# Weight conversion in a fused attention and feed-forward kernel: two of its seven steps on GpSimd, and one chunk later at the start

## The chip, the cores and the metric

The kernel runs on one core of a Trainium2 chip. The core has a matrix engine (TensorE, PE in the profile, its weight loads PEld), a vector engine (VectorE, DVE), a scalar engine (ScalarE, ACT), a third elementwise engine (GpSimd, POOL) and a queue that here issues all DMA transfers (SyncE, SP). The engines run their own instruction streams in order and wait for each other through semaphores. PE writes to PSUM, which POOL does not touch in this kernel; everything else lives in SBUF. The metric is device time in microseconds of one execution; the median of several runs is given.

## The reference

For 8 batches, 8 heads, 576 positions and head size 64, attention with a local mask: the first four heads see the last 32 positions, the other four every fourth of the last 128. The result, laid out as 4608 tokens by 512, goes through a feed-forward layer with a leaky rectifier:

```python
scores = scale * np.matmul(q, k.transpose(0, 1, 3, 2))
scores = np.where(masks[None, :, :, :], scores, -1000000000.0)
attn = softmax(scores)
x = np.matmul(attn, v).transpose(0, 2, 1, 3).reshape(B * S, H * D)
h = x @ w_in                                        # 512 -> 2048
g = np.maximum(h, 0.0) + alpha * np.minimum(h, 0.0)
return (g @ w_out).astype(np.float32)               # 2048 -> 512
```

q, k, v and alpha are 32-bit floats. The weights `w_in` and `w_out` reach the kernel as 64-bit words: each weight is stored as a double.

## The kernel before

**Precision.** Every large product is done as three products of a split operand: a value is cast to the matrix engine's 32-bit format (its high part), and the rest (its low part) is value minus high part. `PASSES` pairs high with high, high with low, low with high.

**Weights.** There are 32 chunks, 16 columns blocks of 128 of `w_in` and 16 row blocks of `w_out`. A chunk is 128 partitions by 512 weights, and arrives as 128 × 1024 32-bit words. `load_weight` issues its transfer, from the SP queue, into one of a few staging buffers. A `Conversion` then makes the 32-bit float and its two parts:

- `magnitude` (line 335): ACT takes the absolute value of the upper word, read as a float (line 342).
- `words` (line 344), four instructions of DVE: a clamp to the range of exponents that can be represented (line 348), a shift and mask (350), the upper word's sign and exponent bits brought in (352), the lower word's bits brought in (354). The last of them frees the staging buffer for the next load.
- `high` (line 358): ACT casts into the high weight tile (line 360).
- `low` (line 362): DVE subtracts (line 363) into the low weight tile.

**Order.** The order in which instructions are emitted is written out by hand, and it is the order in each engine's stream. The list `wq` fixes in which order the chunks are loaded and converted: `load()` and `conversion()` take the next one.

**The head** (lines 820 to 892). Attention is done by pairs of heads; a `Pair` has scores on PE, `maxima` on DVE (line 216: PSUM plus mask into SBUF with the row maximum), exponentials on ACT (228), `divisions` on DVE (235 to 238), transposes on PE, copies on ACT (255), values on PE, and `highs` on ACT (302) and `lows` on DVE (307) that split the result. The loop over s does the first four pairs, one per pass, with one chunk converted in each: words interleaved with the second half of the maxima. A chunk's magnitude comes one pass ahead of its words.

**The first stage** (n = 0 to 7, line 904). Step n does the feed-forward of the first 512 tokens for one block of 128 hidden values: `ffn_h` (PE, line 375), `ffn_relu` (ACT, 383 and 384), `ffn_sum` (DVE, 389), `ffn_high` (ACT, 402), `ffn_low` (DVE, 407), `ffn_y` (PE, 422), beside the attention of one more pair over two steps. Up to two chunks a step are converted: `now` holds the chunks whose words come in this step, `late` those whose low part does. The tuples with eight entries say how many chunks are taken and loaded in each step.

**The second stage** (n from 8, line 974) has the next 512 tokens and the rest of the first 512, one chunk a step, until the last one at about step 22. There the first sums of weights (`combine`, lines 466 and 469, the only work on POOL before the change apart from setting constants) follow in emission order; they serve the later stages, which use combined weights (`Four`, `phase_h`, `phase_y`) and convert nothing.

Of the kernel before, what the change touches and what calls it, by code (L numbers as in the profile page):

```python
# [9 lines left out]
F32 = mybir.dt.float32  # L10
F32R = mybir.dt.float32r
U32 = mybir.dt.uint32
AF = mybir.ActivationFunctionType
ALU = mybir.AluOpType
# [34 lines left out]
F64_LOW = float.fromhex("0x1p-15")  # L49
F64_HIGH = float.fromhex("0x1.dffffep16")  # L50
# [7 lines left out]
def tile_window_attention_prelu_ffn(  # L58
# [11 lines left out]
    nc = tc.nc  # L70
# [256 lines left out]
    class Conversion:  # L327
# [7 lines left out]
        def magnitude(self):  # L335
            i = self.index
            if NC <= i < 2 * CUT and i % 2 == 0:
                self.a = spare_a[i // 2 % 2]
            else:
                self.a = ffp.tile([P, DM], U32, tag="m", name=f"wa{self.id}", bufs=5)  # L340

            nc.scalar.activation(out=self.a.bitcast(F32), in_=self.st[:, :, 1].bitcast(F32), func=AF.Abs)

        def words(self):
            a, af = self.a, self.a.bitcast(F32)
            lo, hi = self.st[:, :, 0], self.st[:, :, 1]
            return [
                lambda: nc.vector.tensor_scalar(
                    out=af, in0=af, scalar1=F64_LOW, scalar2=F64_HIGH, op0=ALU.max, op1=ALU.min),
                lambda: nc.vector.tensor_scalar(  # L350
                    out=a, in0=a, scalar1=3, scalar2=0x3FFFFFFF, op0=ALU.logical_shift_left, op1=ALU.bitwise_and),
                lambda: nc.vector.scalar_tensor_tensor(  # L352
                    out=a, in0=hi, scalar=0xC0000000, in1=a, op0=ALU.bitwise_and, op1=ALU.bitwise_or),
                lambda: nc.vector.scalar_tensor_tensor(
                    out=a, in0=lo, scalar=29, in1=a, op0=ALU.logical_shift_right, op1=ALU.bitwise_or),
            ]
# [3 lines left out]
            nc.scalar.copy(out=self.dst[0], in_=self.a.bitcast(F32))  # L360

        def low(self):
            nc.vector.tensor_tensor(  # L363
                out=self.dst[1], in0=self.a.bitcast(F32), in1=self.dst[0].bitcast(F32), op=ALU.subtract)


# [3 lines left out]
    def ffn_h(t, f, first=0, end=NC):  # L370
        if first == 0:
            ms[t, f] = bank("a", [P, TT], f"h_{t}_{f}")
        for c in range(first, end):
            for n, (a, e) in enumerate(PASSES):
                nc.tensor.matmul(  # L375
                    ms[t, f], lhsT=weight(0, a, f)[:, c * P:(c + 1) * P], rhs=half(t, c)[:, e, :],
                    start=(c == 0 and n == 0), stop=(c == NC - 1 and n == 2))

    def ffn_relu(t, f):

        ps = ms[t, f]
        m = ffp.tile([P, TT], F32, tag="m", name=f"m_{t}_{f}", bufs=5)
        nc.scalar.activation(out=m, in_=ps, func=AF.Relu, scale=-1.0)
        nc.scalar.activation(out=ps, in_=ps, func=AF.Relu)
        ms[t, f] = ps, m
# [23 lines left out]
    def ffn_y(t, f):  # L409
        first = (t, f) in ((0, 0), (0, CUT), (1, 0), (2, CUT))  # L410
        if first:
            ys[t] = [bank("y", [P, TT], f"y_{t}_{f}_{c}") for c in range(NC)]
        g = gs.pop((t, f))
        cut, rest = (t, f) == (0, CUT - 1), t == 0 and f == NF - 1
        last = cut or (t, f) in ((0, NF - 1), (1, NF - 1), (2, CUT - 1))
        if last:
            o = [ffp.tile([P, TT], F32, tag="m", name=f"ob_{t}_{f}_{c}", bufs=5) for c in range(NC)]
        for c in range(NC):
            if rest:
                nc.sync.dma_start(out=o[c], in_=part[c])  # L420
            for n, (a, e) in enumerate(PASSES):
                nc.tensor.matmul(  # L422
                    ys[t][c], lhsT=weight(1, a, f)[:, c * P:(c + 1) * P], rhs=g[:, e, :],
                    start=(first and n == 0), stop=(last and n == 2),
                )
        if not last:
            return
        for c in range(NC):
            if rest:
                nc.vector.tensor_tensor(out=o[c], in0=ys[t][c], in1=o[c], op=ALU.add)  # L430
            elif c % 2:
                nc.vector.tensor_copy(out=o[c], in_=ys[t][c])
            else:
                nc.scalar.copy(out=o[c], in_=ys[t][c])  # L434
            nc.sync.dma_start(
                out=part[c] if cut else outT[c * P:(c + 1) * P, t * TT:(t + 1) * TT], in_=o[c])
# [373 lines left out]
    def load():  # L810
        if loads:
            load_weight(*loads.pop(0))

    def conversion():

        w = Conversion(*convs.pop(0))
        w.magnitude()
        return w
# [15 lines left out]
    for s in range(NC):  # L834
        u = pairs[s]
        pairs[s + NC].load_qk()
        load()
        if s == 0:
            u.maxima()
            u.exponentials(0, 3)  # L840
            w = conversion()
            u.exponentials(3)
            nc.vector.tensor_scalar_mul(nal, al, -1.0)
            nc.vector.tensor_scalar(out=bal, in0=al, scalar1=-1.0, scalar2=1.0, op0=ALU.mult, op1=ALU.add)
            for op in w.words():
                op()
        else:
            u.maxima(w.words())
            u.exponentials()
            pairs[s - 1].highs()  # L850
        w.high()
        u.divisions()
        if s + 1 == NC:
            ffn_h(0, 0, 0, 2)
        u.transposes()
        later = conversion()
        u.copies()
        if s + 2 <= NC:
            pairs[s + 2].scores()
        if s:  # L860
            pairs[s - 1].lows()
        w.low()
        w = later
        u.values()
        pairs[s + NC].load_v()
    u, v = pairs[NC - 1], pairs[NC]
# [3 lines left out]
    now = [conversion(), conversion()]  # L870
# [12 lines left out]
    ffn_relu(0, 0)  # L883
    v.exponentials(4)
    ffn_relu(0, 1)
    for _ in range(3):
        load()
    late, now = now, [conversion(), conversion()]
    for w in late:
# [7 lines left out]
    for p in range(2 * NC, AHEAD):  # L897
        n = EARLY + 2 * (p - 2 * NC)
# [5 lines left out]
    for n in range(CUT):  # L904


        scored, valued, turned = score_at.get(n), value_at.get(n), turn_at.get(n)
        words = [op for ops in zip(*(w.words() for w in now)) for op in ops]
        if scored:
            scored.scores()  # L910
        if valued:
            valued.values()
        if n + 1 == CUT:
            ffn_y(*slices[n - 1])
        if n == 0:
            for f in range(2):
                ffn_sum(*slices[f])
        elif turned:
            ffn_sum(*slices[n])
        ffn_high(*slices[n])  # L920
        if turned:
            turned.divisions()
        for w in late:
            w.low()
        if scored:
            scored.maxima([lambda: ffn_low(*slices[n])] + words)
            ffn_h(*slices[n + 1])
            scored.exponentials(0, 4)
            valued.highs()
            scored.exponentials(4)  # L930
            valued.lows()
        else:
            if valued:
                valued.highs()
                valued.lows()
            if n:
                ffn_h(*slices[n + 1])
            ffn_low(*slices[n])
            for op in words[:4]:
                op()  # L940
        following = None
        if turned:
            following = [conversion() for _ in range((2, 2, 2, 1, 0, 0, 1, 1)[n])]
            if n:

                ffn_relu(*slices[n + 1])
                ffn_sum(*slices[n + 1])
            for op in words[4:]:
                op()
        elif not scored:  # L950
            for op in words[4:]:
                op()
        late = now
        for _ in range((2, 2, 1, 0, 0, 1, 1, 1)[n]):
            load()
        if not turned and n < CUT - 1:
            ffn_relu(*slices[n + 1])
        if turned:
            turned.transposes()
            turned.copies()  # L960
        for w in late:
            w.high()
        now = following if turned else [conversion() for _ in range((2, 2, 2, 1, 0, 0, 1, 1)[n])]
        if 0 < n < CUT - 1:
            ffn_y(*slices[n - 1])
    ffn_relu(*slices[CUT])
# [2 lines left out]
    for k in range(NFP):  # L969
        n = SECOND + 1 + 2 * k + (2 if k > 1 else 0)  # L970
# [3 lines left out]
    for n in range(CUT, NS):  # L974
        scored, valued, divided, turned = (at.get(n) for at in (score_at, value_at, divide_at, turn_at))
# [3 lines left out]
        if n <= SECOND - 2:  # L979
# [17 lines left out]
            late, now = now, [conversion()] if convs else []  # L997
# [115 lines left out]
```

## Time and profile before

| What | Value |
|---|---|
| median of 3 runs | 919.5 us (919.32 to 920.11) |
| the profiled execution's own time | 919.12 us |
| its span in the trace | 917.3 us |
| PE busy | 869.6 us, 95% of the span |
| DVE busy | 549.4 us, 60% |
| ACT busy | 428.1 us, 47% |
| POOL busy | 48.8 us, 5% |
| mean granted TensorE clock | 0.978 |

A profile of this kind shows one execution. The span runs from the first to the last instruction; the execution's own time is 1.8 us longer. Busy shares are means over stages that differ: the conversions end before a quarter of the span is over.

### The profile page before, as it was taken

How to read it: one execution, taken by the hardware profiler on the slowest of the kernel's cores; microseconds unless marked ns; L12 is line 12 of the kernel's file. 1: busy time of each engine (PE TensorE's matmuls, PEld its weight loads, DVE VectorE, ACT ScalarE, POOL GpSimd, SP SyncE). 2: the span in 40 equal slices, each digit the busy share in tenths (PEclk: the TensorE clock that was granted, in tenths of full speed). 3: DMA queues.
4: the chain of work that ended last, by engine and by line, in shares of the span. 5: the costliest groups of instructions: out<-in, count | busy, mean ns of one | idle time of the engine just before them, and what ended most of it. 6: DMA issues, size and time to landing. Idle time of an engine off the chain costs nothing.

```text
span 917.3 us, 20648 instructions
## 1 busy us (share of the span) xinstructions
PE 869.6 (95%) x8080; PEld 714.5 (78%) x8080; DVE 549.4 (60%) x1607; ACT 428.1 (47%) x1250; POOL 48.8 (5%) x54
## 2 busy tenths in 40 slices
PE   4668999979999998999999999999999999999998
PEld 4556888868877886888778877887888888888886
DVE  6999487686766675676345746673347627503731
ACT  6776455453535444365445543554456306303610
POOL 0000000030222541000000000000000000000000
PEclk9879999999999998999999999999999999999999
DMA  9842152216798984475557656665466456435641
GB/s 334 295 138 70 47 189 93 91 53 202 253 305 268 305 277 152 145 209 163 174 176 200 172 179 192 201 173 155 150 165 182 145 161 195 137 103 157 183 132 46
DMA packets 101313, 159.83 MB, mean 174 GB/s; under 512 B 8416, under 2 KB 47456, under 8 KB 101216
## 3 DMA queue, kind: packets, MB, share of 16 engines
q1 hardware_dynamic: 101216, 158.51, 55.8%
q8 instruction: 64, 1.05, 0.5%
q14 instruction: 33, 0.27, 0.1%
HBM read 124.92 MB, written 33.55 MB: 173 GB/s over the span
## 4 chain that ended last, share of the span: by engine, by line
PE 87%; DVE 7%; ACT 2%; DMA 1%; issue 1%; SPq 1%; DVEq 0%; ACTq 0%
PE y L705 28%; PE pA L567 14%; PE h L375 14%; PE y L422 13%; PE pC L567 7%; PE pB L567 4%; PE o L266 3%; PE s L192 3%; PE t L248 2%; DMA ws<-w_in 1%; ACT w_dt.float L228 1%; DVE w_dt.float L216 1%; DVE w_dt.float32r L363 1%; DVE wa L352 0%; DMA w_dt.uint<-w_out 0%
## 5 line engine op out<-in xcount | busy, mean ns | idle before, releaser
L375 PE MATMUL h<-x,w_dt.float32r 128*128 128x512 f32 x576 | 150.7, 414 | 7.3 <-DVE nm L216 6.9
L422 PE MATMUL y<-g,w_dt.float32r 128*128 128x512 f32 x576 | 140.7, 393 | 0.0
L375 PEld LDWEIGHTS h<-x,w_dt.float32r 128*128 128x128 f32 x576 | 114.2, 201 | 33.0 <-issue 7.3
L422 PEld LDWEIGHTS y<-g,w_dt.float32r 128*128 128x128 f32 x576 | 106.6, 188 | 22.4 <-ACT ob L434 0.4
L705 PE MATMUL y<-gp,ring_w 128*128 128x512 f32 x480 | 113.7, 392 | 0.0
L705 PE MATMUL y<-gp,ring_xA 128*128 128x512 f32 x444 | 104.7, 391 | 1.0 <-issue 1.0
L705 PEld LDWEIGHTS y<-gp,ring_w 128*128 128x128 f32 x480 | 89.3, 188 | 18.6
L705 PEld LDWEIGHTS y<-gp,ring_xA 128*128 128x128 f32 x444 | 82.8, 188 | 18.4 <-issue 1.1
L228 ACT ACTIVATE pr<-pr,nm 128x64 f32<-128x64 f32 (+1 forms) x240 | 80.1, 335 | 28.7 <-DVE nm L216 28.7
L609 ACT COPY stage<-pA 128x512 f32<-128x512 f32 x72 | 42.3, 587 | 104.3 <-PE pA L567 104.3
L402 ACT CAST g<-m 128x512 fp32r<-128x512 f32 x48 | 29.8, 621 | 72.5 <-DVE m L397 66.2
L635 DVE TENSOR_TENSOR gp<-n,gp 128x512 fp32r<-128x512 f32 x96 | 63.2, 684 | 0.0
L627 DVE SCALAR_TENSOR_TENSOR n<-n,bal,stage 128x512 f32<-128x512 f32 x72 | 53.9, 749 | 13.9 <-ACT n L623 13.1
L567 PE MATMUL pA<-parts_w,ring_w 128*128 128x512 f32 x234 | 57.7, 390 | 0.0
L631 ACT CAST gp<-n 128x512 fp32r<-128x512 f32 x96 | 56.6, 615 | 1.9 <-DVE n L627 1.9
L567 PE MATMUL pA<-parts_w,ring_xA 128*128 128x512 f32 x228 | 56.2, 390 | 0.5 <-ACT raw_xB L302 0.5
L705 PE MATMUL y<-gp,ring_g 128*128 128x512 f32 x228 | 55.0, 393 | 0.0
L216 DVE CUSTOM_DVE_ANT_0 pr<-s,mask_sb 128x64 f32<-128x64 f32 (+1 forms) x288 | 45.0, 213 | 16.3 <-PE s L192 15.2
L623 ACT ACTIVATE n<-stage 128x512 f32<-128x512 f32 x72 | 45.6, 633 | 12.5 <-DVE stage L616 12.0
L567 PEld LDWEIGHTS pA<-parts_w,ring_w 128*128 128x128 f32 x234 | 43.8, 188 | 9.1
L728 DVE TENSOR_TENSOR ob<-y,py 128x512 f32<-128x512 f32 x24 | 16.4, 691 | 57.4 <-PE y L705 57.4
L567 PEld LDWEIGHTS pA<-parts_w,ring_xA 128*128 128x128 f32 x228 | 42.7, 188 | 9.5 <-ACT raw_xB L302 0.6
(104 smaller groups left out, 1213.5 us busy)
## 6 DMA issues: line engine op xcount, KB each, us to landing
ring_w<-wS SPq DMA_DIRECT2D x68, 256.0 KB, 2.8
ring_xA<-wS SPq DMA_DIRECT2D x67, 256.0 KB, 2.8
v<-vW SPq DMA_DIRECT2D x24, 576.0 KB, 3.9
ring_w<-wO SPq DMA_DIRECT2D x40, 256.0 KB, 2.8
ring_xA<-wO SPq DMA_DIRECT2D x37, 256.0 KB, 2.7
out<-ob SPq DMA_DIRECT2D x36, 256.0 KB, 3.2
ring_g<-wS SPq DMA_DIRECT2D x33, 256.0 KB, 2.8
wO<-w_dt.float32r SPq DMA_DIRECT2D x32, 256.0 KB, 5.2
```

The lines of the kernel that those rows point to most:

```text
L216: nc.vector.tensor_tensor_reduce(out=self.pr[rows, r, :], in0=self.ps[e][rows, g, :], in1=mask_sb[rows, kind, :], scale=-SCALE, scalar=3.0 ...
L228: nc.scalar.activation(out=self.pr[rows, r, :], in_=self.pr[rows, r, :], func=AF.Exp, bias=self.nm[rows, r:r + 1], scale=-1.0, accum_out=s ...
L375: nc.tensor.matmul(ms[t, f], lhsT=weight(0, a, f)[:, c * P:(c + 1) * P], rhs=half(t, c)[:, e, :], start=(c == 0 and n == 0), stop=(c == NC ...
L402: nc.scalar.copy(out=g[:, 0, :], in_=ms[t, f])
L422: nc.tensor.matmul(ys[t][c], lhsT=weight(1, a, f)[:, c * P:(c + 1) * P], rhs=g[:, e, :], start=(first and n == 0), stop=(last and n == 2),)
L567: nc.tensor.matmul(to, lhsT=w[:, (2 * a + c) * P:(2 * a + c + 1) * P], rhs=part_of(name, e)[:, c * TT:(c + 1) * TT], start=start and c == ...
L609: nc.scalar.copy(out=self.s(n), in_=self.A)
L623: nc.scalar.activation(out=self.m[n], in_=self.at(n), func=AF.Relu, scale=-1.0)
L627: nc.vector.scalar_tensor_tensor(out=self.m[n], in0=self.m[n], scalar=bal[:, f:f + 1], in1=self.at(n), op0=ALU.mult, op1=ALU.add)
L631: nc.scalar.copy(out=self.g(n)[:, 0], in_=self.m[n])
L635: nc.vector.tensor_tensor(out=g[:, 1], in0=self.m.pop(n), in1=g[:, 0].bitcast(F32), op=ALU.subtract)
L705: nc.tensor.matmul(ys2[tt], lhsT=w[:, k * P:(k + 1) * P], rhs=g[:, e], start=j == 0 and n == 0, stop=j == GF - 1 and n == 2)
```

## The change

The clamp moves from `words` into `magnitude` and from DVE to POOL, so that it is issued right behind the absolute value; `words` has three instructions now, and slices such as `words[:4]` and `words[:2]` cut at other places in the sequence. The subtraction of the low part moves from DVE to POOL. In the head, pass s = 0 converts nothing any more: chunk 0's magnitude is the one that pass 0 issues for the next pass, and every later chunk of the head and of steps 0 to 2 comes one place later. Step 3 takes two chunks instead of one. One load that was issued ahead of step 0 is issued later, and step 2 issues two loads instead of one, so that from step 4 on the numbers are as before.

```diff
-            nc.scalar.activation(out=self.a.bitcast(F32), in_=self.st[:, :, 1].bitcast(F32), func=AF.Abs)
+            af = self.a.bitcast(F32)
+            nc.scalar.activation(out=af, in_=self.st[:, :, 1].bitcast(F32), func=AF.Abs)
+            nc.gpsimd.tensor_scalar(
+                out=af, in0=af, scalar1=F64_LOW, scalar2=F64_HIGH, op0=ALU.max, op1=ALU.min)
...
             return [
-                lambda: nc.vector.tensor_scalar(
-                    out=af, in0=af, scalar1=F64_LOW, scalar2=F64_HIGH, op0=ALU.max, op1=ALU.min),
...
         def low(self):
-            nc.vector.tensor_tensor(
+            nc.gpsimd.tensor_tensor(
                 out=self.dst[1], in0=self.a.bitcast(F32), in1=self.dst[0].bitcast(F32), op=ALU.subtract)
...
         if s == 0:
             u.maxima()
-            u.exponentials(0, 3)
-            w = conversion()
-            u.exponentials(3)
+            u.exponentials()
             nc.vector.tensor_scalar_mul(nal, al, -1.0)
             nc.vector.tensor_scalar(out=bal, in0=al, scalar1=-1.0, scalar2=1.0, op0=ALU.mult, op1=ALU.add)
-            for op in w.words():
-                op()
         else:
             u.maxima(w.words())
             u.exponentials()
             pairs[s - 1].highs()
-        w.high()
+            w.high()
...
         if s:
             pairs[s - 1].lows()
-        w.low()
+            w.low()
...
-    for _ in range(3):
+    for _ in range(2):
         load()
...
-            following = [conversion() for _ in range((2, 2, 2, 1, 0, 0, 1, 1)[n])]
+            following = [conversion() for _ in range((2, 2, 2, 2, 0, 0, 1, 1)[n])]
...
-        for _ in range((2, 2, 1, 0, 0, 1, 1, 1)[n]):
+        for _ in range((2, 2, 2, 0, 0, 1, 1, 1)[n]):
             load()
...
-        now = following if turned else [conversion() for _ in range((2, 2, 2, 1, 0, 0, 1, 1)[n])]
+        now = following if turned else [conversion() for _ in range((2, 2, 2, 2, 0, 0, 1, 1)[n])]
```

More of the change, by code (lines that the diff above doesn't have):

```diff
@@ L340, in magnitude @@
                 self.a = ffp.tile([P, DM], U32, tag="m", name=f"wa{self.id}", bufs=5)
-            nc.scalar.activation(out=self.a.bitcast(F32), in_=self.st[:, :, 1].bitcast(F32), func=AF.Abs)
+            af = self.a.bitcast(F32)
+            nc.scalar.activation(out=af, in_=self.st[:, :, 1].bitcast(F32), func=AF.Abs)
+            nc.gpsimd.tensor_scalar(
+                out=af, in0=af, scalar1=F64_LOW, scalar2=F64_HIGH, op0=ALU.max, op1=ALU.min)
         def words(self):
-            a, af = self.a, self.a.bitcast(F32)
+            a = self.a
             lo, hi = self.st[:, :, 0], self.st[:, :, 1]
             return [
-                lambda: nc.vector.tensor_scalar(
-                    out=af, in0=af, scalar1=F64_LOW, scalar2=F64_HIGH, op0=ALU.max, op1=ALU.min),
                 lambda: nc.vector.tensor_scalar(
```

## The prediction

> **What bounds the kernel now.** I read the table of busy time by stretch first, because a mean over 917 us hides stages with different limits, then who waited for whom, the chain that ended last inside the stretches that mattered, and the timeline there. The columns of the table: stretch, its length, then busy us and count for PE, PEld, DVE, ACT, POOL, the granted PE clock, DMA share, GB/s.
>
> ```profile
> core 0 of [0], span 917.3 us
> core 0: us, PE busy (x) PEld busy (x) DVE busy (x) ACT busy (x) POOL busy (x), PEclk, DMA share, GB/s
> 21.00:28.00 7.00, 4.29 (x150) 3.65 (x149) 6.20 (x36) 5.98 (x27) 0.00 (x0) 0.92 1.05 388
> 43.00:92.00 49.00, 37.19 (x548) 30.27 (x549) 46.16 (x155) 34.81 (x110) 0.00 (x0) 0.82 0.30 100
> 106.00:183.00 77.00, 77.00 (x368) 63.18 (x360) 58.02 (x102) 40.29 (x75) 0.00 (x0) 1.00 0.38 125
> 183.00:203.00 20.00, 15.30 (x200) 12.28 (x200) 17.62 (x56) 9.16 (x34) 7.08 (x6) 0.95 0.12 31
> ```
> ```profile
> PE h L375 <- DVE nm L216: 5.0, 2, 3.2
> ```
>
> Four stages concern the change, all before 204 us, where the last chunk is converted. In the head (one row of it, 21 to 28) DVE is busy 6.20 of 7.00 us and ACT 5.98. From 43 to 92 DVE is the limit: 46.16 of 49 us, while PE has 12 us of gaps, two of them (5.0 us) because a matmul had to wait for the row maxima of line 216. From 106 to 183 PE has no gap: what DVE saves there is worth nothing, and DVE's 19 us of slack is what may be lost unseen. From 183 to 203 PE has gaps of 4.7 us again. POOL does nothing until 192.
>
> **What is removed, added and moved.** For each of 32 chunks the clamp and the low part go from DVE to POOL; one conversion leaves pass s = 0 of the head, and everything behind it is one chunk later until step n = 3 takes two chunks and catches up. No transfer is added; of the SP queue, one of the three loads ahead of step 0 goes behind it, and one of step 3's into step 2. In each step a load still waits for the same words as before, one chunk earlier in number, so no transfer is newly exposed. The prices of DVE's part, on the chain of the head (start, length, what):
>
> ```profile
> 5.82 8.20 DMA ws<-w_in
> 14.05 0.67 ACT wa L342
> 14.72 0.58 ACT pt L255 x2
> 15.30 3.32 ACT w_dt.float L228 x20
> ...
> 25.89 0.19 DVE rs L235
> ...
> 28.15 0.60 DVE w_dt.float32r L363
> 29.75 0.34 DVE wa L348
> ...
> 33.13 0.19 DVE rs L235
> ```
>
> A clamp takes 0.34 us of the path and a low 0.60, so a chunk frees DVE for 0.94 us. *Head.* A pass lasts 33.13 − 25.89 = 7.24 us, and both pieces lie on its chain. Without them it is 6.3, and ACT's share of the pass (5.98/7.00 × 7.24 = 6.2) becomes nearly equal, so I take a full 0.95 us for each of the passes s = 2 and 3: 1.9 us. The two POOL instructions of a pass fall after the cast of line 360, while DVE subtracts out of PSUM (line 307) or starts its maxima (scores in PSUM), so I charge no contention here. If that cover is missing it costs up to what is gained.
>
> Ahead of that, the first pass. Before, the conversion of chunk 0 stood in it, and chunk 1's magnitude waited at 14.05 for its weights, 8.20 us after their issue; the copies and the 3.32 us of exponentials stood behind it on ACT.
>
> ```profile
> 10.47 0.19 ACT L228 ACTIVATION_READ_ACCUMULATOR w_dt.float<-w_dt.float,nm 64x1 f32 x1
> 10.79 0.17 DVE L235 TENSOR_SCALAR rs<-sums 128x10 f32<-128x10 f32 x1
> ...
> 12.08 1.30 PE L248 MATMUL t<-ident,w_dt.float 128*128 128x128 f32 x5 [0.86 <-DVE w_dt.float L238]
> ```
>
> After, the last exponential ends one magnitude earlier (10.66 − 0.67 ≈ 10.0) and DVE has no words left to finish, so the division starts near 10.05 instead of 10.79. The transposes then end at 13.38 − 0.75 ≈ 12.6, the copies at 13.25, the 3.32 us of exponentials at 16.6; before they ended at 15.30 + 3.32 = 18.62. The magnitude that now stands between is chunk 0's, whose words DVE had finished by 10.79 before, so its weights are there. That is 2.0 us, and DVE (maxima and three words, about 3.3 us from 11.35) is done by then. Here the cost moves: the next pieces of DMA, later in the queue, had no wait before and are asked for 2 to 4 us sooner; with the queues full (388 GB/s) one of them may become late. Sum of the head: 2.0 + 1.9 = **3.9 us** (bounds 1.5, if the transfers pace it, and 4.6).
>
> *43 to 92, the first stage.* The rows of lines 348 and 363 in this stretch (busy us and count in DVE):
>
> ```profile
> 43.00:92.00 49.00, 3.54 (x9) 0.82 0.30 100
> ```
> ```profile
> 43.00:92.00 49.00, 7.80 (x12) 0.82 0.30 100
> ```
>
> Nine clamps and twelve lows leave: 9 × 0.34 + 12 × 0.60 = 10.3 us of DVE. What they cost on POOL: the trace has no POOL clamp and no POOL subtraction with this output, so by the nearest rows:
>
> ```profile
> 299.75 2.54 POOL L466 TENSOR_TENSOR wsum_xA<-w_dt.float32r 128x512 f32<-128x512 f32 x2 [8.60 <-DVE wc L479]
> ```
> ```profile
> masks.py:199 POOL TENSOR_SCALAR_AFFINE_SELECT ident<-ident 128x128 f32<-128x128 f32 x1 | 0.3, 292 | 0.1
> masks.py:197 POOL MEMSET ident<- 128x128 f32 x1 | 0.2, 204 | 0.3 <-POOLq L1106 0.3
> L1106 POOL MEMSET const-bfloat16-1.0<- 128x1 bf16 x1 | 0.1, 101 | 0.0
> ```
>
> A two-input POOL instruction of this shape takes 1.27 us: the low. The clamp has one input: the memset, stretched by its slope from one column to 128, gives 0.10 + 4 × 0.10 = 0.5, the floor; the affine select, which does arithmetic, 0.10 + 4 × 0.19 = 0.87; the two-input row 1.27 is the ceiling. I take 0.87. What decides is not that POOL is slower but what it does to DVE beside it, and the trace shows that once:
>
> ```profile
> 192.97 1.52 DVE L348 TENSOR_SCALAR wa<-wa 128x512 f32<-128x512 f32 x1
> 194.53 1.39 DVE L350 TENSOR_SCALAR wa<-wa 128x512 uint32<-128x512 uint32 x1
> 195.84 1.21 DVE L407 TENSOR_TENSOR g<-m,g 128x512 fp32r<-128x512 f32 x1
> 196.97 1.21 DVE L352 SCALAR_TENSOR_TENSOR wa<-ws,wa 128x512 uint32<-128x512 uint32 x1
> 198.21 1.09 DVE L354 SCALAR_TENSOR_TENSOR wa<-ws,wa 128x512 uint32<-128x512 uint32 x1
> ```
> ```profile
> 192.66 2.98 POOL L466 TENSOR_TENSOR wsum_xB<-w_dt.float32r 128x512 f32<-128x512 f32 x2 [191.36 <-PE t L248]
> 195.72 4.18 POOL L469 TENSOR_TENSOR wsum_xB<-wsum_xB 128x256 f32<-128x256 f32 x4
> ```
> ```profile
> 195.76 0.30 PE L192 MATMUL s<-k,q 64*32 64x64 f32 x2
> 200.75 1.30 PE L192 MATMUL s<-k,q 64*32 64x64 f32 x70 [4.70 <-DVE m L397]
> ```
>
> Five DVE instructions that take some 2.5 us alone (0.34, 0.34, three of 0.60) needed 6.33 us, from 192.97 to 199.30, while POOL ran without a gap; POOL's pair took 2.98 instead of 2.54. So DVE loses (6.33 − 2.5)/6.33 = 0.6 us for each us of POOL beside it. All five read and write SBUF alone. The Trainium skill ("SBUF — State Buffer", section "Who interferes with whom") says that a DVE instruction with two SBUF inputs, or a one-input one in its two-port mode, takes the port pair that GpSimd uses, that the holder keeps it for the whole instruction and the other waits. The trace agrees that they exclude each other (a clamp of 0.34 took 1.52); it differs in the price, as DVE lost 0.6 of POOL's time and not all of it.
>
> Instructions with an operand in PSUM I take as free of this (none stands beside POOL in those rows). Their busy time from 58 to 75, lines 216, 307 and 389:
>
> ```profile
> 58.00:75.00 17.00, 2.18 (x24) 0.90 0.35 119
> ```
> ```profile
> 58.00:75.00 17.00, 0.89 (x3) 0.90 0.35 119
> ```
> ```profile
> 58.00:75.00 17.00, 1.48 (x2) 0.90 0.35 119
> ```
>
> That is 4.6 us of DVE's 17; without clamps and lows (3.8) some 13 remain, of which 65% contend. POOL's time there, slowed as the pair above (1.49 a low, about 1.0 a clamp): 9 × 1.0 + 12 × 1.49 = 26.9 us; 26.9 × 0.65 × 0.6 = 10.5 us lost against 10.3 saved. On top, the words of one chunk more fall into this stage, as the head has one chunk fewer (step 4 gets two instead of one): 0.34 + 2 × 0.60 = 1.5 us of DVE, of which I charge 1.0, since DVE has 2.8 us idle in the stage. Sum of the stage: **−1.2 us**. Bounds: +6 if POOL meets mostly maxima, −11 if DVE is blocked at nearly every POOL instruction.
>
> *106 to 183.* DVE has 19 us spare over 14 chunks, 1.4 us each, and gets 0.94 more against 2.5 × 0.6 = 1.5 us lost at most. Nothing.
>
> *183 to 203.* Here POOL's order matters. The sums of line 466 are the first thing in POOL's queue now and start as soon as their buffer is free, at 192.66, beside the words of the last chunk; PE then waits 4.70 us for line 397 behind them. After the change POOL must do the last chunk's low first, and that waits for the high part, which waits for exactly those words. So the sums can't start before the words are over. DVE gains the 3.8 us lost above, and 0.34 + 0.34 + 0.60 from clamps and low; against it one low part of 1.27 us blocks the shift of the last chunk by about 1.2. I get 3.8 + 1.3 − 1.2 = 3.9, near PE's gap of 4.7, and take **3.8 us** (bounds 2.0 and 4.7). The sums then run some 5 us later, beside maxima and PSUM work, and are needed two steps later: nothing.
>
> Sum: 3.9 − 1.2 + 3.8 = 6.5 us off the profiled execution's own 919.12 (span 917.3): 912.6. The runs' median, 919.5, lies 0.4 above it, so **913.0 us**.
>
> **Rivals.** *Blocked for the whole instruction*: uncontended POOL time 9 × 0.87 + 12 × 1.27 = 23.1 us × 0.65 = 15 us lost against 10.3, and 1.0: −5.7; the head stays, the last stage gives 3.2. Net 1.4: 918.1. For it: the clamp's row of 1.52. Against: the two-input rows, 1.1 to 1.2. The rule of the Trainium skill cited above would have it so.
>
> *Slower.* The same place, with a dear clamp: if POOL needs 1.49 for it too and the lows come just when DVE does words (casts finish right after a chunk's words, so its low meets the next chunk's), then POOL works 21 × 1.49 = 31.3 us, all of it beside contending work: 31.3 × 0.6 = 18.8 lost, 10.3 saved, 1.0 more: −9.5; with 7.7 from head and end that is 1.8 us slower, about 921.5. It decides from a loss of 7.7 us in the first stage on, which is 0.37 us for each of its 21 moved instructions beyond what the move saves. Against it: each scored step has twelve maxima of 0.2 us under which POOL can run.
>
> *The stage gains too.* If lows and clamps fall mostly under maxima, 43 to 92 gives 6 us instead of losing: 905.5. For it: POOL starts a low as soon as the cast ends, and maxima follow the casts in every other step.
>
> *It doesn't do what it says*: DVE would wait for clamps at its first word if POOL lay behind. A clamp is issued most of a step before its word; I fold it into the slower case.
>
> **Chances and range.** Forecast 0.56 (909 to 916.5 by the bounds of head and end), whole-instruction blocking 0.18, slower 0.12, gain in the stage too 0.14. What can be told from no change is 0.2%, 1.8 us. Faster: 0.56 + 0.14 and a third of 0.18, 0.76; within: 0.11, the middle of the blocking case; slower: 0.13. The range goes from 905 to 920, with both outer cases' near ends.
>
> **What would show it.** Right: the division of pair 3 near 29.3 instead of 33.13; no wait of ACT for the second weights; line 350, 352 and 354 longer than 0.6 to 1.2 us beside POOL and unchanged elsewhere; the first sums of line 466 after 195 us, and PE's wait of 4.70 us below 1.5. Wrong: a POOL clamp above 1.3 us, first-stage steps longer than 8.5 us, or PE gaps between 106 and 183. The forecast falls if 43 to 92 loses more than 4 us.

## The result, and the profile after

The changed kernel takes 927.93 us (median of 5 runs, 925.69 to 931.3), the kernel before 919.5 us beside it (5 runs): a ratio of 1.0095, 95% interval 1.0067 to 1.0122. The forecast was 913.0 us, with a range up to 920. It is slower by 8.4 us where 6.5 us of gain were forecast. The profiled execution is the fastest of the five: 925.69 us, span 923.9 us, against 919.12 and 917.3 before, so the trace shows 6.6 us of the loss. Medians here and below are over all executions; the ratios leave out one, of the kernel with the clamp on DVE, which took 4835.98 us where its other three took 908.98 to 911.12.

The table of busy time by stretch, after the change, over the same stretches as in the prediction (length, then busy us and count of PE, PEld, DVE, ACT, POOL, granted clock, DMA share, GB/s):

```profile
21.00:28.00 7.00, 4.04 (x108) 3.44 (x116) 6.01 (x27) 4.42 (x18) 2.14 (x3) 1.00 1.05 390
43.00:92.00 49.00, 33.95 (x383) 26.96 (x383) 42.91 (x107) 30.17 (x96) 28.84 (x18) 0.72 0.31 98
106.00:183.00 77.00, 77.00 (x405) 63.39 (x404) 52.83 (x73) 41.13 (x81) 38.15 (x23) 0.99 0.34 112
183.00:203.00 20.00, 20.00 (x157) 16.36 (x156) 14.78 (x45) 12.37 (x36) 10.39 (x7) 1.00 0.25 83
```

From 43 to 92 us PE does less than before (33.95 us instead of 37.19), and so does DVE (42.91 instead of 46.16). DVE gets 107 instructions done there and not 155, at 0.40 us each in the mean instead of 0.30, and is idle for 6.1 us instead of 2.8. So two things may be at work: something makes DVE wait, and something makes its instructions longer. From 106 to 183 PE still has no gap. The last row lies earlier in the work than it did before, because the same steps now come later.

Four marks that both traces have cut the difference into parts: the division of pair 3 at the end of the head; the first matmul of the scores in step 20, ahead of the last chunk's stage; the same for the next pair's scores behind that stage; and the end of the span. (Starts in us, as the view of the chain gives them; the last four rows of the table are the lengths between.)

| | before | after | difference |
|---|---|---|---|
| pair 3's division | 33.13 | 33.41 | +0.3 |
| scores of step 20 | 183.21 | 195.25 | +12.0 |
| scores behind the last chunk | 216.31 | 223.90 | +7.6 |
| end of the span | 917.3 | 923.9 | +6.6 |
| head | 33.13 | 33.41 | +0.3 |
| first stage and on to step 20 | 150.08 | 161.84 | **+11.8** |
| last chunk's stage | 33.10 | 28.65 | **−4.4** |
| the rest | 701.0 | 700.0 | −1.0 |

So the end of the conversions gave about what was forecast (4.4 us, 3.8 forecast), and the loss lies in front of it. What is new there is on POOL. The groups of the two moved instructions, by shape (count, busy us, mean ns; then POOL's idle time before them):

```profile
L344 POOL TENSOR_SCALAR wa<-wa 128x512 f32<-128x512 f32 x26 | 52.9, 2035 | 74.6 <-ACT wa L343 74.6
L364 POOL TENSOR_TENSOR w_dt.float32r<-wa,w_dt.float32r 128x512 fp32r<-128x512 f32 x26 | 35.1, 1350 | 4.1 <-ACT w_dt.float32r L361 4.1
```

The clamp takes 2.04 us, half as long again as the subtraction with its two inputs. And DVE waits for it, 17.8 us in all up to 215 us, of which 5.8 lie between 20 and 106 us (the view of waits: who for whom, us, times, longest):

```profile
DVE wa L351 <- POOL wa L344: 17.8, 16, 1.7
```

How that looks once in the head, first on POOL and then on DVE (start, length):

```profile
19.14 1.92 POOL L344 TENSOR_SCALAR wa<-wa 128x512 f32<-128x512 f32 x1 [6.39 <-ACT wa L343]
21.02 1.27 POOL L364 TENSOR_TENSOR w_dt.float32r<-wa,w_dt.float32r 128x512 fp32r<-128x512 f32 x1
```
```profile
21.09 1.49 DVE L351 TENSOR_SCALAR wa<-wa 128x512 uint32<-128x512 uint32 x1 [1.47 <-POOL wa L344]
```

DVE stands still for 1.47 us, until the clamp ends. Then POOL starts the subtraction that stood behind the clamp, 0.07 us before DVE starts the shift, and the shift takes 1.49 us instead of 0.42. The chain of waits goes through POOL here, where POOL did nothing at all in the kernel before (start, length, whose):

```profile
26.50 0.58 ACT wa L343
...
27.16 1.93 POOL wa L344
...
34.88 0.57 ACT wa L343
...
35.53 1.92 POOL wa L344
37.44 1.23 POOL w_dt.float32r L364
38.67 2.06 POOL w_dt.float L344
40.73 1.89 POOL wa L344
```

In the last chunk's stage the prediction nearly holds. POOL must do the chunk's low part first, and the sums of weights (now line 467) start after the words are over; PE, then, waits 1.60 us and not 4.70 for the split behind those words, and the 12 matmuls of `h` that follow take 3.04 us where they took 4.16 (after on POOL and PE, then PE before):

```profile
208.97 1.27 POOL L364 TENSOR_TENSOR w_dt.float32r<-wa,w_dt.float32r 128x512 fp32r<-128x512 f32 x1 [2.94 <-ACT w_dt.float32r L361]
210.19 2.98 POOL L467 TENSOR_TENSOR wsum_xB<-w_dt.float32r 128x512 f32<-128x512 f32 x2
```
```profile
209.68 0.95 PE L192 MATMUL s<-k,q 64*32 64x64 f32 x70 [1.60 <-DVE m L398]
210.71 3.04 PE L376 MATMUL h<-x,w_dt.float32r 128*128 128x512 f32 x12
```
```profile
201.98 4.16 PE L375 MATMUL h<-x,w_dt.float32r 128*128 128x512 f32 x12
```

### The profile page after: what moved, and what is told of

Its sections match the earlier page's. It is cut to its first block, busy times and chain, and to the rows that moved or that the text cites. A ratio compares the mean times of both kernels' runs of the same rounds, so it can differ in the third digit from the quotient of the medians.

```text
span 923.9 us, 20689 instructions
## 1 busy us (share of the span) xinstructions
PE 876.3 (95%) x8080; PEld 719.5 (78%) x8080; DVE 549.5 (59%) x1543; ACT 430.1 (47%) x1250; POOL 154.4 (17%) x118
## 4 chain that ended last, share of the span: by engine, by line
PE 84%; DVE 5%; ACT 3%; POOL 2%; issue 2%; DMA 2%; SPq 0%; DVEq 0%; ACTq 0%; POOLq 0%
PE y L706 28%; PE pA L568 14%; PE h L376 12%; PE y L423 12%; PE pC L568 7%; PE pB L568 4%; PE o L266 4%; PE s L192 2%; POOL wa L344 2%; PE t L248 1%; DMA w_dt.float<-kT 1%; DMA ws<-w_in 1%; DVE w_dt.float L353 1%; DVE wa L353 1%; POOL w_dt.float L344 1%
## 5 line engine op out<-in xcount | busy, mean ns | idle before, releaser
L376 PE MATMUL h<-x,w_dt.float32r 128*128 128x512 f32 x576 | 152.6, 418 | 6.2 <-DVE nm L216 3.4
L706 PEld LDWEIGHTS y<-gp,ring_xA 128*128 128x128 f32 x444 | 82.8, 188 | 18.1 <-issue 0.9
L344 POOL TENSOR_SCALAR wa<-wa 128x512 f32<-128x512 f32 x26 | 52.9, 2035 | 74.6 <-ACT wa L343 74.6
L628 DVE SCALAR_TENSOR_TENSOR n<-n,bal,stage 128x512 f32<-128x512 f32 x72 | 54.0, 749 | 13.9 <-ACT n L624 13.3
L729 DVE TENSOR_TENSOR ob<-y,py 128x512 f32<-128x512 f32 x24 | 16.4, 691 | 57.4 <-PE y L706 57.4
```

The lines of the kernel that those rows point to most:

```text
L344: nc.gpsimd.tensor_scalar(out=af, in0=af, scalar1=F64_LOW, scalar2=F64_HIGH, op0=ALU.max, op1=ALU.min)
L376: nc.tensor.matmul(ms[t, f], lhsT=weight(0, a, f)[:, c * P:(c + 1) * P], rhs=half(t, c)[:, e, :], start=(c == 0 and n == 0), stop=(c == NC ...
L628: nc.vector.scalar_tensor_tensor(out=self.m[n], in0=self.m[n], scalar=bal[:, f:f + 1], in1=self.at(n), op0=ALU.mult, op1=ALU.add)
L706: nc.tensor.matmul(ys2[tt], lhsT=w[:, k * P:(k + 1) * P], rhs=g[:, e], start=j == 0 and n == 0, stop=j == GF - 1 and n == 2)
```

## The experiments

Three causes were on the table. **A**: the clamp on POOL is dear, and its length lies on the path between absolute value and shift. **B**: the subtractions block DVE, as the prediction's rival "blocked for the whole instruction" had it. **C**: the new order, one chunk later, is at fault. Times are medians, each ratio is against the kernel before on the same chip, with its 95% interval.

### One part at a time

The changed kernel with only the clamp back on DVE:

```diff
-            nc.gpsimd.tensor_scalar(
-                out=af, in0=af, scalar1=F64_LOW, scalar2=F64_HIGH, op0=ALU.max, op1=ALU.min)
...
             return [
+                lambda: nc.vector.tensor_scalar(
+                    out=af, in0=af, scalar1=F64_LOW, scalar2=F64_HIGH, op0=ALU.max, op1=ALU.min),
```

> The changed kernel with the clamp back on DVE as the first of four words; the low parts stay on POOL and the chunks one place later. Theory A (the POOL clamp's own time, 1.92 us, makes DVE wait at the shift behind it, 17.8 us in all, and that is the loss): the first stage gets back most of its 12 us, the sums behind the last chunk stay late, so 912 to 917. Theory B (POOL's lows block DVE's words, whatever the clamp does): still above 923. Theory C (the later order of chunks costs the time): about 926.

911.0 us, ratio 0.9896 (0.9876 to 0.9916): 17 us faster than the changed kernel. B alone is out: all 32 subtractions on POOL make the kernel faster.

The changed kernel with only the subtraction back on DVE:

```diff
-            nc.gpsimd.tensor_tensor(
+            nc.vector.tensor_tensor(
                 out=self.dst[1], in0=self.a.bitcast(F32), in1=self.dst[0].bitcast(F32), op=ALU.subtract)
```

> The changed kernel with the low parts back on DVE; only the clamp is on POOL. Theory A: 922 or more, and DVE still waits for the clamp ahead of line 351, about 15 us. Theory B: 914 to 918, as nothing with two inputs runs on POOL beside the words any more, and shifts are back near 0.42 us. Theory C: about 926.

924.77 us, ratio 1.0048 (1.0032 to 1.0064). The clamp alone costs, and the wait is there without any subtraction on POOL:

```profile
DVE wa L351 <- POOL wa L344: 14.5, 15, 1.8
```

Both edits together, so that the new order alone is left:

> Clamp and low both back on DVE; what is left of the change is the order, one chunk later. Theories A and B: 2 to 3 us faster than before, 916.5 to 918, from the first pass of the head (its division already stands near 9.8 instead of 10.8, the second pass's near 16.4 instead of 18.6). Theory C: 922 or more.

919.06 us, ratio 0.9992 (0.9979 to 1.0006). C is out: the order by itself costs nothing. By the end it gives nothing that can be told from no change either, where 2 to 3 us were expected. And the other way about, both parts on POOL in the old order (the kernel before with the changed kernel's `magnitude`, `words` and `low`):

> The kernel before with clamp and low moved to POOL and the old order of chunks kept. Theories A and B: the first pass's gain is missing as well, 929 to 932. Theory C: 915 to 918, the gain of the move without the loss of the order.

930.16 us, ratio 1.0111 (1.0081 to 1.0141). That is the changed kernel's ratio within the two intervals, so the new order isn't what makes the move dear.

The start of step 20's scores makes a table of the four ways to place the two parts, all in the new order, each from one trace:

| | clamp on DVE | clamp on POOL |
|---|---|---|
| low part on DVE | 182.55 | 188.87 (+6.3) |
| low part on POOL | 179.72 (−2.8) | 195.25 (+12.7) |

The two edits don't add: −2.8 and +6.3 would make +3.5, and it is +12.7, 9.2 us more. That is taken up again below.

### How long the clamp is

If A holds, the time must follow the clamp's length. Three kernels change that alone. One leaves the upper limit out, so that the instruction has one operation instead of two; one clamps only 200 of the 512 columns and leaves 312 as they are; one does the whole clamp in two instructions of 256 columns.

```diff
-                out=af, in0=af, scalar1=F64_LOW, scalar2=F64_HIGH, op0=ALU.max, op1=ALU.min)
+                out=af, in0=af, scalar1=F64_LOW, scalar2=None, op0=ALU.max)
```

> The changed kernel with half a clamp: POOL's instruction has only the lower limit (the upper limit is left out). If the price of a POOL clamp goes by its operations, it falls from 1.92 to about 1 us, DVE's wait ahead of the shift all but goes, and the time is 912 to 918. If it goes by elements alone, 1.9 us and 925 to 929 as with the full clamp.

```diff
-                out=af, in0=af, scalar1=F64_LOW, scalar2=F64_HIGH, op0=ALU.max, op1=ALU.min)
+                out=af[:, :200], in0=af[:, :200], scalar1=F64_LOW, scalar2=F64_HIGH, op0=ALU.max, op1=ALU.min)
```

> The changed kernel with the POOL clamp over the first 200 of 512 columns alone (the other 312 are left unclamped), which should bring its price down to about the 0.87 us that the prediction took. If the price of the clamp is the one term that was mis-sized, the rest of the prediction's sum holds: 911 to 915, and DVE's wait ahead of the shift falls from 17.8 us to under 4. If having any POOL instruction between magnitude and shift is the trouble (a handover more, or the block by the low behind it), 919 or more.

```diff
-                out=af, in0=af, scalar1=F64_LOW, scalar2=F64_HIGH, op0=ALU.max, op1=ALU.min)
+                out=af[:, :256], in0=af[:, :256], scalar1=F64_LOW, scalar2=F64_HIGH, op0=ALU.max, op1=ALU.min)
+            nc.gpsimd.tensor_scalar(
+                out=af[:, 256:], in0=af[:, 256:], scalar1=F64_LOW, scalar2=F64_HIGH, op0=ALU.max, op1=ALU.min)
```

> The changed kernel with each POOL clamp as two instructions of 256 columns. What the clamp's price is made of: if a fixed part dominates, each half takes well over 0.96 us and the pair over 2.4; if columns do, 1.0 each and about 2.0 for the pair, and the time stays within 2 us of the changed kernel's 928. No theory expects a gain.

The groups of the clamp by shape, one operation, 200 columns, and the two halves:

```profile
L344 POOL TENSOR_SCALAR wa<-wa 128x512 f32<-128x512 f32 x26 | 43.2, 1662 | 81.3 <-ACT wa L343 78.2 <-ACT w_dt.float32r L360 3.1
```
```profile
L344 POOL TENSOR_SCALAR wa<-wa 128x200 f32<-128x200 f32 x26 | 25.1, 967 | 92.4 <-ACT wa L343 79.4 <-DVE nm L216 7.7 <-DVE x L307 5.2
```
```profile
L344 POOL TENSOR_SCALAR wa<-wa 128x256 f32<-128x256 f32 x26 | 32.1, 1234 | 69.7 <-ACT wa L343 57.9 <-DVE nm L216 6.7 <-DVE x L307 5.2
...
L346 POOL TENSOR_SCALAR wa<-wa 128x256 f32<-128x256 f32 x26 | 27.9, 1074 | 0.0
```

| clamp on POOL | mean us of it | median us | ratio |
|---|---|---|---|
| 200 of 512 columns | 0.97 | 911.57 | 0.991 (0.9891 to 0.9928) |
| one operation | 1.66 | 921.55 | 1.0025 (1.0012 to 1.0038) |
| the changed kernel | 2.04 | 927.93 | 1.0095 (1.0067 to 1.0122) |
| two halves | 1.23 + 1.07 | 929.21, one run | |

The clamp with one operation came out between the two cases that were expected, 1 us and 1.9. In the kernel with 200 columns DVE's wait for clamps fell to 8.0 us and not under 4, but 7.5 of them lie between 106 and 183 us, where PE is full.

The time follows the length: from 0.97 to 2.04 us it grows by 16.4 us, 15 us for each us of a clamp. POOL does 14 clamps between 20 and 92 us in the changed kernel (the groups of that stretch):

```profile
L344 POOL TENSOR_SCALAR wa<-wa 128x512 f32<-128x512 f32 x8 | 16.1, 2011 | 16.5 <-ACT wa L343 16.5
...
L344 POOL TENSOR_SCALAR w_dt.float<-w_dt.float 128x512 f32<-128x512 f32 x6 | 12.5, 2090 | 20.2 <-ACT w_dt.float L343 20.2
```

So with the subtractions on POOL as well, it is as if every clamp of head and first stage lay on the path with its whole length. That is a description and no mechanism: with the subtractions on DVE, a clamp of some 2 us on POOL adds 5.7 us to the time (919.06 to 924.77), under 3 us for each us. With the clamp of 0.97 us, near the 0.87 that the prediction assumed, the kernel is at 911.6 us, where 913.0 was forecast.

### Where the clamp costs

Clamps of the first 18 chunks on DVE, of the last 14 on POOL, all subtractions on POOL:

```diff
+            if i >= 18:
+                self.clamp(nc.gpsimd)
...
+            first = [] if self.index >= 18 else [lambda: self.clamp(nc.vector)]
```

> The changed kernel with the clamp on POOL only for the last 14 chunks, those converted while PE has no gaps; the first 18 clamp on DVE. If the loss lies in the first stage alone and DVE's slack later takes the waits, 911 to 913 (the last chunk's clamp may cost 1 to 2 us, as its shift waited 1.2 us in the changed kernel). If a POOL clamp of 1.92 us costs wherever it stands, 917 or more.

911.15 us, ratio 0.9917 (0.9896 to 0.9937), as with no clamp on POOL at all (911.0). DVE waits for these clamps three quarters as long as in the changed kernel:

```profile
DVE wa L357 <- POOL wa L349: 13.3, 10, 1.4
```

Of these 13.3 us 12.2 lie between 106 and 183 us, where PE is full, and cost nothing. Of the 17.8 us of the changed kernel, 8.2 lie between 106 and 183 us and are free for the same reason. The sum of a wait over a whole trace says little; its place decides.

### The last chunk's low part alone

The kernel before, with one of its 32 subtractions on POOL, the last:

```diff
-            nc.vector.tensor_tensor(
+            (nc.gpsimd if self.index == 2 * NF - 1 else nc.vector).tensor_tensor(
```

> The kernel before with one single instruction moved: the low part of the last chunk goes to POOL, in front of the sums of line 466 in POOL's queue. If holding back those sums is what the last stage gains, PE's gap of 4.7 us ahead of 201 us falls to about 1.5 and the time is 3 us shorter, 916 to 917.5, with nothing changed before 183 us. If the gain needs the other lows off DVE too, less than 1 us: 919 to 920.

913.59 us, ratio 0.9941 (0.9921 to 0.9961). One moved instruction holds back the sums of line 466, and PE's wait falls from 4.70 to 1.18 us. The order on POOL and, behind the wait, PE with `h` at 3.01 us instead of 4.16:

```profile
196.56 1.27 POOL L363 TENSOR_TENSOR w_dt.float32r<-wa,w_dt.float32r 128x512 fp32r<-128x512 f32 x1 [195.26 <-ACT w_dt.float32r L360]
197.78 2.99 POOL L466 TENSOR_TENSOR wsum_xB<-w_dt.float32r 128x512 f32<-128x512 f32 x2
```
```profile
197.26 0.95 PE L192 MATMUL s<-k,q 64*32 64x64 f32 x70 [1.18 <-DVE m L397]
198.29 3.01 PE L375 MATMUL h<-x,w_dt.float32r 128*128 128x512 f32 x12
```

By the scores behind the stage the kernel is 4.9 us ahead (211.46 against 216.31). That is the prediction's last term, shown by itself, and more than the 3 us that were expected. The median lies 6.4 us under the 920.0 of the kernel before; for what goes beyond the 4.9 no run shows a cause.

### Why the head gave nothing

With the clamp on DVE, the copies of the first pair's transposes started 2.6 us sooner, at 12.07 us, sooner even than was forecast. But the first values product (line 266) did not follow. The kernel before, then the changed kernel with its clamp on DVE:

```profile
16.07 2.14 PE L266 MATMUL o<-pt,w_dt.float 64*64 64x32 f32 x72 [1.25 <-ACT w_dt.float L228]
```
```profile
16.29 2.14 PE L266 MATMUL o<-pt,w_dt.float 64*64 64x32 f32 x72 [2.39 <-ACT w_dt.float L228]
```

The view names ACT as the releaser, with a wait that is longer now though ACT was sooner. The operand left over is the pair's values, which come by DMA; no view names their transfer here. To see whether it is them, the first weight chunk's load was moved behind the loads that this product needs:

```diff
-    load()
...
+    load()
```

(one line, from ahead of the second pair's q and k to behind them and the first pair's values; the rest as with the clamp on DVE)

> The kernel with the clamp on DVE and the lows on POOL, and the load of chunk 0 issued behind those of pair 1 and of pair 0's values. In all runs so far the first product with the values starts at 15 to 16.3 us, whether its other operand is ready at 13 or at 15.3; if the full transfer queue sets that, it starts near 14.7 now, the head ends 1 to 1.4 us sooner, and the time is 909.5 to 910.5. If not, 911 as without the reordering, or 1 us more if chunk 0's weights become late.

908.29 us, ratio 0.9889 (0.9869 to 0.9909), and the product starts 1.6 us sooner:

```profile
14.68 2.15 PE L266 MATMUL o<-pt,w_dt.float 64*64 64x32 f32 x72 [0.49 <-ACT w_dt.float L228]
```

Pair 3's division comes at 29.93 us instead of 31.10. In the traces of all the kernels that load in the old order the product starts between 15.06 and 16.29 us, whenever the copies end. So 14.68 lies outside, but how much of the 1.6 us is the moved load is not shown; nor is it separated whether it is the values or the second pair's q and k, which moved up too. That transfers hold up this product, and the head with it, is what fits best; they come at 390 GB/s in the first table's row. This is the lowest median found, 1.1% under the kernel before, with the subtractions on POOL and the clamps on DVE; its interval overlaps that of the same kernel with the loads in the old order.

### Why the two parts together cost 9 us more

Two ideas were tried. The first: POOL starts a subtraction just as its clamp releases the shift (21.02 and 21.09 us above), so the collision is built in. Here every subtraction is issued right behind its cast and the clamps behind the subtractions:

```diff
+        def clamp(self):
+            af = self.a.bitcast(F32)
...
         for w in late:
             w.high()
+            w.low()
...
+        for w in now:
+            w.clamp()
```

> The changed kernel with both parts on GpSimd, but each chunk's subtraction issued on GpSimd right behind the cast that it follows, ahead of the clamps that follow in the list, so that no subtraction stands directly behind the clamp that releases a shift. Theory that the extra 9 us of the two parts together come from the subtraction that GpSimd starts just as its clamp releases VectorE's shift: a part of it comes back, a mean shift well under the 1.25 us of the changed kernel and 919 to 924 us. Rival, that only the length of VectorE's wait for its clamps counts: the clamps come later behind the subtractions, the wait grows from 17.8 us, and the time is 928 us or more.

945.86 us, ratio 1.0291 (1.0264 to 1.0318). The collision at the shift is gone, a shift of the main group (the 26 chunks with their floats in `wa`) takes 0.49 us and not 1.25, but the wait grows from 17.8 to 57.4 us:

```profile
DVE wa L354 <- POOL wa L347: 47.3, 21, 3.3
...
DVE w_dt.float L354 <- POOL w_dt.float L347: 10.1, 5, 3.1
```

The chain shows why: POOL's queue is in order, and now each pair of clamps stands behind a pair of subtractions (two subtractions, then the first clamp of the pair).

```profile
53.43 3.15 POOL w_dt.float32r L367 x2
56.59 1.88 POOL w_dt.float L347
```

So this kernel trades the collision for a longer wait, and says only that the wait costs more. What the collision costs by itself it doesn't show.

The second idea was a ring. In the changed kernel ACT waits for subtractions, because chunks 8 and 12 write their floats where chunks 4 and 8 had theirs (43 to 92 us; with only one of the two parts on POOL it is 0.4 and 0.8 us):

```profile
ACT w_dt.float L343 <- POOL w_dt.float32r L364: 7.2, 2, 4.1
```

So these two chunks got other space, which pairs 4 and 5 have left by then:

```diff
-                self.a = spare_a[i // 2 % 2]
+                self.a = rooms[i // 4 - 2][:, :DM].bitcast(U32) if i in (8, 12) else spare_a[i // 2 % 2]
```

> The changed kernel, with its clamps and subtractions on GpSimd in the same order, but the floats of chunks 8 and 12 written into space that two earlier pairs of heads have left, instead of the buffers of chunks 4 and 8. In the changed kernel ScalarE waits 7.2 us in two pieces (3.08 and 4.11) for the subtractions that free these buffers; with only one of the two parts on GpSimd it waits 0.4 and 0.8 us. Theory that the 9 us which the two parts cost together beyond their sum are this ring (a subtraction queued on GpSimd behind two clamps, the next absolute value behind it, its clamp behind that): the two waits vanish, the scores of step 20 start near 188 to 190 us instead of 195.25, and the time is 919 to 923 us. Rival, that they come from VectorE blocked at its shifts and from the wait for clamps: 926 to 930 us as before.

928.41 us, ratio 1.0087 (1.0062 to 1.0113): no change. ACT's wait is gone and comes back one instruction later, at the cast, which waits for the words (15.1 us between 20 and 106 us, 7.9 in the changed kernel):

```profile
ACT w_dt.float32r L361 <- DVE w_dt.float L355: 15.1, 3, 6.3
```

So the buffers are not it. Nor is the granted clock from 43 to 92 us, 0.72 in the changed kernel: it is 0.79 here and 0.79 in the kernel with the order alone, whose step 20 begins 14.5 us sooner.

The blocked instructions are not ruled out, and the traces speak for them. The shift of the main group between 20 and 92 us, in the changed kernel, with the clamp on DVE, and with the subtraction on DVE (count, busy us, mean ns; then DVE's idle time before it):

```profile
L351 DVE TENSOR_SCALAR wa<-wa 128x512 uint32<-128x512 uint32 x8 | 10.7, 1338 | 4.7 <-POOL wa L344 4.7
```
```profile
L351 DVE TENSOR_SCALAR wa<-wa 128x512 uint32<-128x512 uint32 x9 | 3.7, 415 | 0.1
```
```profile
L351 DVE TENSOR_SCALAR wa<-wa 128x512 uint32<-128x512 uint32 x9 | 4.6, 508 | 7.2 <-POOL wa L344 7.2
```

With the clamp alone on POOL the wait, 7.2 us, is about what is lost (6.3). With both parts the wait is smaller, and the instructions are longer. Summed over all groups of DVE between 20 and 106 us, against the mean times in the kernel with the order alone, they are longer by 18.1 us in the changed kernel, by 6.5 with only the subtraction on POOL and by 3.2 with only the clamp there. That is 8.4 us more than the two single moves together, near the 9.2 that were to be explained. With the clamp on 200 columns it is 12.4 us, and the wait is 0.5. Not all of this lies on the path, and no run takes the collision away without lengthening the wait. POOL's queue may have a part of its own: in the changed kernel it runs four clamps and four subtractions without a gap from 52.70 to 66.40 us, two clamps behind two subtractions behind two clamps. How the 9 us divide stays open.

## Why the prediction was wrong

**The step that failed** is the price of the POOL clamp: "the two-input row 1.27 is the ceiling. I take 0.87." It measured 1.92 us undisturbed and 2.04 in the mean, beyond the ceiling. The bound rested on the assumption that a one-input instruction can't be dearer than a two-input one of the same shape, which no row showed. The kernel with 200 columns tests the sum at about the assumed price: from pair 3's division to step 20 it takes 183.06 − 31.66 = 151.4 us against 150.08 before, a loss of 1.3 us where the stage was put at 1.2, and its time is 911.6. With the true length the same stretch loses 11.8. That 911.6 lies so near the forecast of 913.0 is in part luck: in its trace the head gives 1.5 us and not 3.9, the last chunk's stage 5.7 and not 3.8, and the rest of the span is 3.5 us shorter, which the sum doesn't have.

**The wait that was waved away** goes with it: "A clamp is issued most of a step before its word; I fold it into the slower case." It was issued early but ran late, for ACT's absolute value itself comes close before the words (26.50 in the chain above, the clamp to 29.09, the shift then), and in the first stage a clamp queues behind subtractions. The rival "slower" (0.12) put its mechanism in DVE's losses beside POOL, with a clamp of 1.49, and its condition, a first-stage loss above 7.7 us, came true. Those losses are there (18.1 us of longer instructions between 20 and 106 us, for 50.9 us of POOL), and DVE's wait at its first word comes to 5.8 us in the same stretch; it was named and given no price.

**Head, −3.9 us of time**: +0.3. The order alone moved pair 3's division from 33.13 to 31.78, 1.35 us, close to the bound of 1.5 "if the transfers pace it". That transfers hold it up fits the moved load, though one trace carries it; then the wrong choice was to take the engines' chain and leave the DMA as a bound. The clamp on POOL took that back (32.19 without, 33.41 with the subtractions). The divisions, where 29.3 was to show the forecast right:

```profile
9.83 0.17 DVE L235 TENSOR_SCALAR rs<-sums 128x10 f32<-128x10 f32 x1 [1.52 <-ACT w_dt.float L228]
16.37 0.17 DVE L235 TENSOR_SCALAR rs<-sums 128x10 f32<-128x10 f32 x1 [1.11 <-ACT w_dt.float L228]
25.39 0.17 DVE L235 TENSOR_SCALAR rs<-sums 128x10 f32<-128x10 f32 x1 [0.77 <-ACT w_dt.float L228]
33.41 0.17 DVE L235 TENSOR_SCALAR rs<-sums 128x10 f32<-128x10 f32 x1 [0.77 <-ACT w_dt.float L228]
```

The first two come sooner, as worked out; the passes after them, 9.0 and 8.0 us instead of 7.24, are longer, not shorter.

**First stage, +1.2 us of time**: near for a clamp of the assumed price, but by a rate that did not hold. "0.6 us for each us of POOL beside it" is not what subtractions alone do. In the kernel with the clamp on DVE, between 43 and 92 us, it is POOL that is stretched; DVE's words are as long as ever:

```profile
L364 POOL TENSOR_TENSOR w_dt.float32r<-wa,w_dt.float32r 128x512 fp32r<-128x512 f32 x7 | 17.1, 2442 | 5.6 <-ACT w_dt.float32r L361 5.6
```
```profile
L355 DVE SCALAR_TENSOR_TENSOR wa<-w_dt.uint,wa 128x512 uint32<-128x512 uint32 x6 | 4.1, 684 | 0.0
L349 DVE TENSOR_SCALAR w_dt.float<-w_dt.float 128x512 f32<-128x512 f32 x5 | 4.0, 796 | 0.0
...
L235 DVE TENSOR_SCALAR rs<-sums 128x10 f32<-128x10 f32 x3 | 2.6, 853 | 0.0
```

What DVE loses is in instructions that start just behind a subtraction: this clamp takes 0.80 us in the mean instead of 0.41, a division 0.85 instead of 0.17, the subtraction of line 408 0.88 instead of 0.68, the short product of line 238 0.63 instead of 0.28. Five, three, six and three of them make 5 × 0.39 + 3 × 0.68 + 6 × 0.20 + 3 × 0.35 = 6.2 us, for 24.8 us of POOL (with six subtractions of the other buffer, 7.7 us): 0.25, not 0.6. The row of 192 to 199 us that gave 0.6 had POOL's queue filled without a gap, and with the subtractions alone that was not the case. With both parts on POOL the rate is 18.1/50.9 = 0.36.

**106 to 183 us, nothing**: right. PE has no gap (77.00 of 77.00) although DVE waits 8.2 us for clamps there.

**The last chunk's stage, −3.8 us**: right in its mechanism, 4.4 in the changed kernel and 4.9 with the one subtraction moved. The number is near for partly another reason: PE's wait shrinks by 3.1 us (4.70 to 1.60, and not below the 1.5 that was to show the forecast right), and the `h` behind it is 1.1 us shorter, which the prediction did not count.

## What to carry to other kernels

A row of another operation bounds a price only from the side that a reason gives: fewer inputs did not make an instruction cheaper on another engine, and an instruction without a row should have its worst price in the range wherever it stands between two others on the path. Work moved to a slow idle engine pays when nothing waits for it soon (here the low part, above all the last one) and costs time when it is a link in a chain that another engine waits on (the clamp), however much time it frees. Where a head is full of transfers, ask what they deliver and in which order before counting what the engines save.

## What was unexpected of the hardware

- A POOL instruction with one input and two operations on 128 × 512 floats takes 1.92 us, dearer than the subtraction with two inputs (1.27). With one operation it is 1.49 us, on 200 columns 0.88, so 3.3 ns for a column ((1.92 − 0.88)/312). DVE needs 0.41 us for the clamp and 0.68 for the subtraction, so POOL takes 4.7 times and 1.9 times as long. The Trainium skill ("GPSIMD Engine Reference", section "4.1 Engine selection") puts two-input operations at about twice VectorE's time and one-input ones at roughly line rate. The first agrees with the runs (1.9 times), the second does not for this clamp (4.7 times).

```profile
26.47 0.88 POOL L344 TENSOR_SCALAR wa<-wa 128x200 f32<-128x200 f32 x1 [4.86 <-ACT wa L343]
```
```profile
19.89 1.49 POOL L344 TENSOR_SCALAR wa<-wa 128x512 f32<-128x512 f32 x1 [7.50 <-ACT wa L343]
```

- Who is blocked, DVE or POOL, depends on who comes first. A subtraction that started 0.07 us ahead of DVE's shift made the shift take 1.49 us (above). One that started while DVE was at work took 3.65 us itself: it ended at 44.38, 1.13 us after the last of four words that followed each other on DVE, none of them lengthened (the kernel with the clamp on DVE; POOL, then DVE):

```profile
40.73 3.65 POOL L364 TENSOR_TENSOR w_dt.float32r<-wa,w_dt.float32r 128x512 fp32r<-128x512 f32 x1 [5.58 <-ACT w_dt.float32r L361]
```
```profile
39.47 1.39 DVE L307 TENSOR_TENSOR x<-o,x 128x256 fp32r<-128x256 f32 x4
40.75 0.70 DVE L353 SCALAR_TENSOR_TENSOR w_dt.float<-w_dt.uint,w_dt.float 128x512 uint32<-128x512 uint32 x1
...
42.55 0.70 DVE L355 SCALAR_TENSOR_TENSOR wa<-w_dt.uint,wa 128x512 uint32<-128x512 uint32 x1
```

  The Trainium skill ("SBUF — State Buffer", section "Who interferes with whom") says that the order of issue decides who blocks, and for the whole instruction. Both rows agree; in the second DVE kept POOL out over several instructions in a row, not one.
